# One PSUM bank and one copy for a chunk's value products, four score banks, spread-out maxima, and a new order for the attention stage

## The chip, the cores and the metric

The kernel runs on one core of one Trainium2 chip. The metric is the device time of one execution in microseconds (us). The kernel before took 383.84 us, the median of three runs (383.47, 383.84 and 385.26 us).

## The reference, cut to what matters

Three stages follow each other. Everything is float32, but `moe2_w_in` and `moe2_w_out`, which arrive as 8-byte floats and are converted on the chip.

```
q, k, v: (4 batches, 8 heads, 576 positions, 64)
scores = q k^T / 8                      # masked: heads 0-3 a window of the last 32 positions,
                                        # heads 4-7 every 4th of the last 128 positions
attn   = softmax(scores) ; a = attn v   # a, reordered: x of shape (2304, 512)
logits = x phi (512 x 32)               # softmax over all 2304 rows -> 32 slots of 512
slots  -> 8 experts: relu(slot w1) w2   # w1 8x512x1024, w2 8x1024x512
y      = softmax(logits, over slots) slot_out
out    = relu(y w_in)^2 w_out           # w_in 512x2048, w_out 2048x512
```

## The kernel before, in words

The changed part is the attention stage. It walks 24 **chunks**. A chunk is a pair of **units** (a unit is two heads of one batch) and a third of the positions: three blocks of 64 queries, each against 96 keys. Three chunks make a pair of units, six make a batch. A chunk has two **groups** (one for each head of the units), and these steps, each named by a letter:

- `q` (ch_qk, L342): the mask and the scores of both groups, one PSUM bank each. The pool `ps_s` has three banks, so the second of the next chunk's two score banks comes free only when the first group of the chunk has been exponentiated.
- `m` (ch_max, L366), once for each group: VectorE takes the row maxima, three numbers a row, negated.
- `c` (ch_sc, L372): VectorE multiplies the six maxima of a chunk by the scale 0.125, in place (L374).
- `x` (ch_exp, L376), once for each group: ScalarE's three exponentials (L381) with their sums.
- `r` (ch_rec, L386): VectorE adds 1e-9 to the six sums in place (L387) and takes the reciprocals (L388).
- `n` (ch_norm, L390), once for each group: the product with the reciprocals (L392), on GpSimd (`.g`) or VectorE (`.v`).
- `t` and `T`, once for each group: TensorE transposes (L400) into the one bank of `ps_t`, ScalarE or VectorE copies it out (L405).
- `p` (ch_pv, L408), once for each *unit*: the value products (L414) into a bank of `ps_v`, which has two banks.
- `P` (ch_pvev, L422), once for each unit: the copy into the ring `xring` of single-unit tiles, one copy (L432) for the window heads, two strided ones (L439) for the dilated heads.
- `d` (dup_v, L224), once for each unit of a chunk: 32 rows of v are copied to other partitions (L230), all by GpSimd.

When the six chunks of a batch are through, the router's work on the batch follows in the same queues: `X`/`Xe` transpose a unit's result (L452) and copy it out (L467), `L`, `Le`, `Lx`, `L2`, `D`, `De`, `Dx` make the logits and their exponentials, `S`/`Se` collect the slots, and `ce`, `cx`, `cn`, `cg` the second softmax.

The order of all this is written out by hand or by a planner in the string `ATT`: each engine executes its part of the tokens in exactly that order, and a token that waits holds up all that stand behind it on its engine. A token without a number takes the next of its kind, `t#27` is group 27. The last letter of a token chooses the engine or the PSUM pool. After the attention, `CL` closes the pools and issues the loads of the first chunks of `w_in` and `w_out` on the SP queue; the experts (`y`, L746, and `x`, L956) and the last stage (L1125, L1129, L1169, L1173) follow, by the string `SEQ`.

The loads are issued on the SP queue in a fixed order (P0, P1, P2, two w1 tiles, P3, two w1 tiles, ...; P is a pair's q, k and v), each as soon as a slot of the ring is free. `q` and `p` of a pair's last chunk free its slots for the weights of the experts.

Of the kernel before, what the change touches and what calls it, by code (L numbers as in the profile page):

```python
# [23 lines left out]
SCALE = 0.125  # L24
# [24 lines left out]
d Xe.a t r cx X.m m n.g T.a p m Xe.a c p n.g cn x t P.v S cg T.v x X.m d P.v q Se d Xe.v t r m X.m n.g T.a p m Xe.a
c p n.g P.v x t P.v S d x T.v q Se d t r X.m m n.g T.a p m Xe.a p c n.g P.v x t P.v p T.v x p d P.v q P.v d t r m S  # L50
n.g T.a m L c Se n.g x t#27 x Le q d T#27.v d Lx X.m r m t#26 n.g Xe.a p m T#26.a c X.m n.g L2.v x t P.v D Xe.v p x
De q d T.v P.a X.m r Dx m t n.g Xe.a m p T.a c n.g p ce x t P.v d S P.v x T.v q Se d cx t r p m n.g T.a m p P.a c
X.m n.g cn x t Xe.v X.m d p T.v x q P.v cg Xe.v P.a d t r p m n.g T.a m S P.a c n.g t x Se X.m d T.v X.m p Xe.v x q
# [39 lines left out]
def attn_softmoe_relu2_kernel(  # L93
# [84 lines left out]
    xring = [(ap1 if i < 4 else aq1).tile([128, S], F32, name=f"xr{i}") for i in range(6)]  # L178
# [45 lines left out]
    def dup_v(u, c):  # L224
# [5 lines left out]
        nc.gpsimd.tensor_tensor(  # L230
            v[:WIN, lo:3 * c + 3, :], v[QB:KB, lo - 1:3 * c + 2, :],
            zero[QB:KB, :n].unsqueeze(2).to_broadcast([WIN, n, 128]), op=ALU.subtract,
        )
# [132 lines left out]
    def ch_max(g):  # L366
        if g % 2 == 0:
            ng_t[g // 2] = ap3.tile([128, 12], F32, tag="ns", name="ns")
        ns = ng_t[g // 2]
        nc.vector.tensor_reduce(ns[:, 3 * (g % 2):3 * (g % 2) + 3], s_t[g], axis=AX.X, op=ALU.max, negate=True)  # L370

    def ch_sc(n):  # L372
        ng = ng_t[n][:, 0:6]
        nc.vector.tensor_scalar(ng, ng, SCALE, None, op0=ALU.mult)  # L374

    def ch_exp(g):  # L376
        p = p_t[g] = app.tile([128, 3, KB], F32, tag="p", name="p")
        ns, a = ng_t[g // 2], 3 * (g % 2)
        s, ng, sm = s_t.pop(g), ns[:, a:a + 3], ns[:, a + 6:a + 9]
        for i in range(3):  # L380
            nc.scalar.activation(  # L381
                p[:, i, :], s[:, i, :], AF.Exp, bias=ng[:, i:i + 1], scale=SCALE, accum_out=sm[:, i:i + 1]
            )
# [24 lines left out]
    def ch_pv(g):  # L408
        n, i = divmod(g, 2)
        u, c = units_of[n][i], units_of[n][2]  # L410
        o = ps_v.tile([128, 3, QB], F32, tag="v", name="o")
        for j in range(3):
            for h in range(2):
                nc.tensor.matmul(  # L414
                    o[64 * h:64 * h + 64, j, :],
                    lhsT=v_t[u][:, 3 * c + j, 64 * h:64 * h + 64],
                    rhs=pt_t[2 * n + h][:, j, QB * i:QB * i + QB],
                    start=True, stop=True,
                )
        pv_t[g] = o  # L420
        if c == 2:
            free(("load_kv", u))  # L422

    def ch_pvev(g, e):
        n, i = divmod(g, 2)
        u, c = units_of[n][i], units_of[n][2]
        b, kc = units[u]
        x = xT_t[b, kc] = xring[u % 6]
        o = pv_t.pop(g).rearrange("p i q -> p (i q)")
# [214 lines left out]
    def glob_w2():  # L644
# [712 lines left out]
```

## Time and profile before

| What | us |
|---|---|
| median of three runs | 383.84 |
| profiled execution | 382.7 |
| its span | 380.8 |
| busy TensorE / VectorE / ScalarE / GpSimd | 364.0 / 317.3 / 244.8 / 78.2 |
| first scores to the last attention exponential | 8.3 to 99.3 |
| first matmul of the experts | 114.9 |

The profiled execution took 382.7 us, of which 380.8 are the span from the first to the last instruction. The attention stage fills the first 105 us, the closing of the router some 9 more, the experts run to 143.6, and the rest is the last stage. TensorE's modelled busy time counts the pipeline's latency, so that 100% is not TensorE at its peak.

### The profile page before, as it was taken

How to read it: one execution, taken by the hardware profiler on the slowest of the kernel's cores; microseconds unless marked ns; L12 is line 12 of the kernel's file. 1: busy time of each engine (PE TensorE's matmuls, PEld its weight loads, DVE VectorE, ACT ScalarE, POOL GpSimd, SP SyncE). 2: the span in 40 equal slices, each digit the busy share in tenths (PEclk: the TensorE clock that was granted, in tenths of full speed). 3: DMA queues.
4: the chain of work that ended last, by engine and by line, in shares of the span. 5: the costliest groups of instructions: out<-in, count | busy, mean ns of one | idle time of the engine just before them, and what ended most of it. 6: DMA issues, size and time to landing. Idle time of an engine off the chain costs nothing.

```text
span 380.8 us, 9512 instructions
## 1 busy us (share of the span) xinstructions
PE 364.0 (96%) x3650; PEld 289.7 (76%) x3650; DVE 317.3 (83%) x681; ACT 244.8 (64%) x663; POOL 78.2 (21%) x161
## 2 busy tenths in 40 slices
PE   7878999999998998999999999999999999999995
PEld 3456777777763333777788788778999999999995
DVE  1768888988773237899999999999899999999984
ACT  3557787778644006899998686656966556465640
POOL 2788887674301020000000000120000000000000
PEclk9999999999999999999999999999999999999999
DMA  7999999998899999484753001300100101010101
GB/s 202 386 389 387 391 391 389 376 333 294 297 367 357 386 382 387 151 314 129 256 184 111 2 0 55 112 0 3 55 2 19 39 2 56 2 57 0 56 1 57
DMA packets 34460, 70.20 MB, mean 184 GB/s; under 512 B 2416, under 2 KB 6256, under 8 KB 34416
## 3 DMA queue, kind: packets, MB, share of 16 engines
q1 hardware_dynamic: 34272, 69.48, 50.9%
q8 instruction: 29, 0.48, 0.5%
q10 hardware_dynamic: 144, 0.13, 0.1%
q14 instruction: 15, 0.12, 0.1%
HBM read 64.88 MB, written 4.72 MB: 183 GB/s over the span
## 4 chain that ended last, share of the span: by engine, by line
PE 65%; DVE 16%; ACT 8%; DMA 4%; issue 4%; SPq 1%; POOL 1%; POOLq 0%; ACTq 0%; DVEq 0%
PE acc L1169 17%; PE acc L1173 8%; PE acc L1125 6%; PE o L414 4%; PE pt L400 4%; PE ph L1059 4%; ACT p L381 3%; DMA wi<-in_w_in_dram 3%; PE acc L1129 3%; PE pso L956 3%; PE xnp L452 2%; PE s L357 2%; DVE lo L1110 2%; PE psh L746 2%; PE ph L1008 2%
## 5 line engine op out<-in xcount | busy, mean ns | idle before, releaser
L1110 DVE TENSOR_TENSOR lo<-g,hi 128x896 fp32r<-128x896 f32 (+2 forms) x75 | 65.4, 873 | 3.3 <-ACT hi L1103 1.2
L1125 PE MATMUL acc<-hl,hi 128*128 128x512 f32 x256 | 67.8, 397 | 0.1
L1069 ACT ACTIVATE u<-ph 128x512 f32<-128x512 f32 (+1 forms) x75 | 42.3, 576 | 25.5 <-PE ph L1059 25.2
L381 ACT ACTIVATE p<-s,ns 128x96 f32<-128x96 f32 x144 | 46.8, 344 | 17.8 <-DVE ns L374 16.9
L1125 PEld LDWEIGHTS acc<-hl,hi 128*128 128x128 f32 x256 | 46.5, 188 | 10.1 <-ACT hi L1103 0.3
L1083 ACT ACTIVATE g<-u 128x512 f32<-128x512 f32 (+1 forms) x67 | 41.4, 620 | 13.9 <-DVE lo L1110 13.1
L1169 PE MATMUL acc<-hl,hi 128*128 128x256 f32 x296 | 48.7, 282 | 0.0
L1169 PEld LDWEIGHTS acc<-hl,hi 128*128 128x128 f32 x296 | 41.2, 188 | 0.0
L1169 PE MATMUL acc<-home,hi 128*128 128x256 f32 x219 | 40.2, 283 | 0.0
L1129 PE MATMUL acc<-hl,lo 128*128 128x512 f32 x128 | 38.0, 400 | 0.0
L700 POOL COPY c3n<-c_all 96x96 f32<-96x96 f32 x24 | 7.8, 359 | 131.6 <-PE ph L712 109.3
L1103 ACT CAST hi<-g 128x512 fp32r<-128x512 f32 (+2 forms) x40 | 29.9, 747 | 7.6 <-DVE g L1094 4.8
L392 POOL TENSOR_TENSOR p<-p,ns 128x288 f32<-128x288 f32 x43 | 27.9, 667 | 21.5 <-DVE ns L388 14.2
L1169 PEld LDWEIGHTS acc<-home,hi 128*128 128x128 f32 x219 | 32.3, 189 | 0.0
L1173 PE MATMUL acc<-hl,lo 128*128 128x256 f32 x148 | 30.2, 282 | 0.0
L381 ACT ACTIVATION_READ_ACCUMULATOR p<-s,ns 128x1 f32 x144 | 30.2, 210 | 0.0
L1129 PEld LDWEIGHTS acc<-hl,lo 128*128 128x128 f32 x128 | 23.4, 188 | 5.6 <-issue 0.4
L400 PE MATMUL pt<-ident,p 128*96 128x128 f32 x144 | 25.1, 283 | 0.9 <-POOL p L392 0.6
L1173 PE MATMUL acc<-home,lo 128*128 128x256 f32 x102 | 24.1, 282 | 0.0
L370 DVE TENSOR_REDUCE ns<-s 128x3 f32<-128x288 f32 x48 | 19.5, 442 | 5.4 <-PE s L357 5.4
L1093 DVE TENSOR_TENSOR g<-g 128x384 f32<-128x384 f32 x39 | 21.5, 552 | 2.7 <-ACT g L1083 2.5
L1173 PEld LDWEIGHTS acc<-hl,lo 128*128 128x128 f32 x148 | 23.6, 189 | 0.0
(217 smaller groups left out, 755.9 us busy)
## 6 DMA issues: line engine op xcount, KB each, us to landing
slotB<-in_w_dram SPq DMA_DIRECT2D x15, 1024.0 KB, 9.7
slotC<-in_w_dram SPq DMA_DIRECT2D x11, 1024.0 KB, 10.3
slotA<-in_w_in_dram SPq DMA_DIRECT2D x6, 1024.0 KB, 6.0
slotA<-in_w_out_dram SPq DMA_DIRECT2D x6, 1024.0 KB, 5.1
slotA<-in_w_dram SPq DMA_DIRECT2D x5, 1024.0 KB, 9.7
out_dram<-o SPq DMA_DIRECT2D x8, 512.0 KB, 2.8
slotC<-in_kq_dram SPq DMA_DIRECT2D x14, 288.0 KB, 8.2
slotB<-in_kq_dram SPq DMA_DIRECT2D x10, 288.0 KB, 9.8
```

The source lines that it names most:

```text
L381: nc.scalar.activation(p[:, i, :], s[:, i, :], AF.Exp, bias=ng[:, i:i + 1], scale=SCALE, accum_out=sm[:, i:i + 1])
L392: {"v": nc.vector, "g": nc.gpsimd}[e].tensor_tensor(p, p, rs.unsqueeze(2).to_broadcast([128, 3, KB]), op=ALU.mult)
L400: nc.tensor.transpose(pt[:, i, :], p[:, i, :], ident)
L1069: nc.scalar.activation(r, u_t[k][:, :n], AF.Relu)
L1083: nc.scalar.activation(out, r, AF.Square)
L1093: E.tensor_tensor(runs(g, 128, 384, 3, 128), runs(g, 0, 384, 3, 128), runs(g, 384, 384, 3, 128), op=ALU.add)
L1103: on(e.lower())(hi[:, :c.stop - c.start], g_t[k][:, c])
L1110: nc.vector.tensor_tensor(lo[:, :n], g_t.pop(k)[:, c], hi_t[k][:, :n], op=ALU.subtract)
L1125: nc.tensor.matmul(a, lhsT=hi_t[k][:, sl], rhs=hl_t[q][:, x, j], start=(fs[0] == 0 and i == 0 and x == 0), stop=False)
L1129: nc.tensor.matmul(a, lhsT=lo_t[k][:, sl], rhs=hl_t[q][:, 0, j], start=False, stop=(fs[-1] == 15 and i == len(fs) - 1))
L1169: nc.tensor.matmul(a, lhsT=hi_t[k][:, sl], rhs=right(q, w, x), start=(q == 0 and x == 0 and i == 0), stop=False)
L1173: nc.tensor.matmul(a, lhsT=lo_t[k][:, sl], rhs=right(q, w, 0), start=False, stop=(q == (6 if p == LP and nm != "Z" else 7) and i == len(PR ...
```

## The change

`ps_s` gets four banks and `ps_v` one. `p` now runs both units' products into one bank (24 matmuls in one run), `P` copies both with one copy (or two strided ones), into ring tiles that hold two units. `c` writes the six scaled maxima to another place of the same tile, as three pairs four columns apart, and the exponentials take their biases from there; `r` writes its sums through that place too, and the reciprocals go back. `d` can be done by ScalarE (`.a`), and 23 of 48 are. `q` chooses its pool by token. The order is written anew, with every token numbered.

```
+q#0.s m#0 m#1 c#0 x#0 q#1.s x#1 q#2.m m#2 d#4.g d#2.a r#0 W d#0.a m#3 d#5.g n#0.v d#1.a d#3.a n#1.g t#1 c#1 m#4 x#3
+m#5 T#1.v x#2 c#2 t#0 x#5 T#0.v d#6.g r#1 p#0 x#4 n#2.g P#0.v q#3.s d#8.g d#7.a r#2 t#2 d#10.a n#3.g m#6 T#2.a m#7
+q#4.s n#4.g d#9.a c#3 t#3 x#7 m#8 n#5.g T#3.v q#5.m x#6 d#11.g m#9 t#4 m#10 m#11 p#1 c#4 T#4.a r#3 d#12.g x#9 t#5
...
...
-    ps_s = att.enter_context(tc.tile_pool(name="ps_s", bufs=3, space=PSUM))
+    ps_s = att.enter_context(tc.tile_pool(name="ps_s", bufs=4, space=PSUM))
-    ps_v = att.enter_context(tc.tile_pool(name="ps_v", bufs=2, space=PSUM))
+    ps_v = att.enter_context(tc.tile_pool(name="ps_v", bufs=1, space=PSUM))
-    xring = [(ap1 if i < 4 else aq1).tile([128, S], F32, name=f"xr{i}") for i in range(6)]
+    xring = [(ap1 if i < 2 else aq1).tile([128, 2, S], F32, name=f"xr{i}") for i in range(3)]
...
+        if e == "a":
+            nc.scalar.copy(dst, src)
+        else:
+            nc.gpsimd.tensor_tensor(
+                dst, src, zero[QB:KB, :n].unsqueeze(2).to_broadcast([WIN, n, 128]), op=ALU.subtract,
+            )
...
+    def pairs_of(n):
+        return ng_t[n][:, 12:24].rearrange("p (a b) -> p a b", b=4)[:, :, 0:2]
     def ch_sc(n):
-        ng = ng_t[n][:, 0:6]
-        nc.vector.tensor_scalar(ng, ng, SCALE, None, op0=ALU.mult)
+        nc.vector.tensor_scalar(pairs_of(n), ng_t[n][:, 0:6], SCALE, None, op0=ALU.mult)
...
-        rs = ng_t[n][:, 6:12]
-        nc.vector.tensor_scalar(rs, rs, 1e-9, None, op0=ALU.add)
-        nc.vector.reciprocal(rs, rs)
+        rs, r2 = ng_t[n][:, 6:12], pairs_of(n)
+        nc.vector.tensor_scalar(r2, rs, 1e-9, None, op0=ALU.add)
+        nc.vector.reciprocal(rs.rearrange("p (a b) -> p a b", b=2), r2)
...
+    def ch_pv(n):
+        u0, u1, c = units_of[n]
+        o = pv_t[n] = ps_v.tile([128, 2, 3 * QB], F32, tag="v", name="o")
+        for i, u in enumerate((u0, u1)):
+            for j in range(3):
+                for h in range(2):
+                    nc.tensor.matmul(
+                        o[64 * h:64 * h + 64, i, QB * j:QB * j + QB],
+                        lhsT=v_t[u][:, 3 * c + j, 64 * h:64 * h + 64],
+                        rhs=pt_t[2 * n + h][:, j, QB * i:QB * i + QB],
+                        start=True, stop=True,
+                    )
+            if c == 2:
+                free(("load_kv", u))
+    def ch_pvev(n, e):
+        u0, u1, c = units_of[n]
+        x = xring[u0 // 2 % 3]
...
+        if units[u0][1] < 2:
+            on(e)(x[:, :, lo:hi], o)
             return
...
+            dst = x.rearrange("p i (t r) -> p i t r", r=DIL)[:, :, t0:t0 + z - a, r]
+            on(e)(dst, o[:, :, a - lo:z - lo])
```

Of the tokens that choose an engine, the new order has these numbers (before in brackets): `n` on VectorE 1 (5), `T` on ScalarE 25 of 48 (24), `Xe` on ScalarE 14 of 32 (16), `L2` on ScalarE 4 of 4 (1), `P` on ScalarE 5 of 24 (12 of 48, each half as large), `d` on ScalarE 23 of 48 (0). In VectorE's order before, `c` of every chunk stood behind `r` of the chunk before it. In the new order it stands ahead of that `r` for 12 of 23 chunks (2, 4, 5, 6, 7, 9, 11, 12, 15, 17, 20, 23) and behind it for the others.

## Rows read from the trace of the kernel before

**Rows 1.** The page: modelled TensorE busy tenths and HBM traffic, 40 slices of 9.52 us.

```profile
PE  7878999999998998999999999999999999999995
GB/s 202 386 389 387 391 391 389 376 333 294 297 367 357 386 382 387 151 314 129 256 184 111 2 0 55 112 0 3 55 2 19 39 2 56 2 57 0 56 1 57
```

**Rows 2.** Windows: stretch, its length, then busy us (instructions) of each engine.

```profile
8.30:47.75 39.45, 33.89 (x568) 23.61 (x568) 29.73 (x89) 26.04 (x135) 31.75 (x56) 1.00 1.04 387
47.75:99.30 51.55, 50.67 (x999) 39.59 (x999) 45.70 (x151) 42.43 (x213) 34.15 (x57) 1.00 0.96 344
99.30:105.50 6.20, 6.20 (x105) 4.58 (x104) 4.11 (x14) 3.31 (x10) 1.61 (x3) 1.00 1.04 370
```

**Rows 3.** ScalarE's waits from 8 to 48 us: total us, times, longest.

```profile
ACT p L381 <- DVE ns L374: 14.9, 10, 5.8
ACT pts L405 <- PE pt L400: 4.3, 9, 0.7
```

**Rows 4.** ScalarE's waits from 48 to 100 us.

```profile
ACT pts L405 <- PE pt L400: 5.2, 8, 1.0
ACT p L381 <- DVE ns L374: 2.4, 7, 0.4
ACT xn L467 <- PE xnp L452: 0.9, 2, 0.5
```

**Rows 5.** Timeline around chunk 2: start us, us, instruction, [idle before it].

```profile
13.85 0.17 DVE L387 TENSOR_SCALAR ns<-ns 128x6 f32<-128x6 f32 x1 [0.76 <-ACT p L381]
14.49 0.90 DVE L392 TENSOR_TENSOR p<-p,ns 128x288 f32<-128x288 f32 x1
15.79 0.31 DVE L374 TENSOR_SCALAR ns<-ns 128x6 f32<-128x6 f32 x1
16.20 0.34 ACT L381 ACTIVATE p<-s,ns 128x96 f32<-128x96 f32 x1 [1.51 <-DVE ns L374]
```

**Rows 6.** The line L374: ns minimum/median/maximum of one instruction.

```profile
L374 DVE TENSOR_SCALAR ns<-ns x24: 170/190/841, 8.0 to 97.0; 128x6 f32<-128x6 f32 x24
```

**Rows 7.** The group of L374 by line: busy us, mean ns of one, idle before.

```profile
L374 DVE TENSOR_SCALAR ns<-ns 128x6 f32<-128x6 f32 x24 | 8.3, 346 | 0.8
```

**Rows 8.** Timelines of GpSimd and VectorE around one slow L374, and GpSimd's first copy.

```profile
73.11 1.29 POOL L392 TENSOR_TENSOR p<-p,ns 128x288 f32<-128x288 f32 x2 [1.05 <-DVE ns L388]
73.78 0.65 DVE L374 TENSOR_SCALAR ns<-ns 128x6 f32<-128x6 f32 x1
...
10.06 1.39 POOL L230 TENSOR_TENSOR slotC<-slotC,zero 32x256 f32<-32x256 f32 x2 [5.54 <-DMA slotC<-in_vw_dram]
```

**Rows 9.** ScalarE's groups from 8.3 to 99.3 us: busy us, mean ns of one.

```profile
L405 ACT COPY pts<-pt 96x384 f32<-96x384 f32 x22 | 10.4, 474 | 9.5 <-PE pt L400 9.4
L439 ACT COPY xr<-o 128x144 f32<-128x144 f32 (+2 forms) x9 | 2.5, 372 | 0.0
L432 ACT COPY xr<-o 128x192 f32<-128x192 f32 x5 | 1.6, 327 | 0.1
L546 ACT ACTIVATE lc<-lc 96x192 f32<-96x192 f32 x3 | 1.1, 375 | 0.0
```

**Rows 10.** Timeline of VectorE: one copy of a window chunk's two, a dilated chunk's four.

```profile
51.91 0.31 DVE L432 COPY xr<-o 128x192 f32<-128x192 f32 x1
55.11 0.85 DVE L439 COPY xr<-o 128x144 f32<-128x144 f32 x4 [0.17 <-PE o L414]
```

**Rows 11.** The line L405: ns minimum/median/maximum of one copy.

```profile
L405 DVE COPY pts<-pt x24: 537/550/555, 12.5 to 102.7; 96x384 f32<-96x384 f32 x24
```

**Rows 12.** The chain that ended last, behind the attention: start us, us, what.

```profile
105.75 12.17 DMA wi<-in_w_in_dram
122.16 0.49 ACT hs L761
```

**Rows 13.** The SP queue's own waits: total us, times, longest.

```profile
SPq L247 <- PE s L357: 10.4, 1, 10.4
SPq L247 <- PE o L414: 7.9, 3, 6.5
```

More of the change, by code (lines that the diff above doesn't have):

```diff
@@ L49 @@
[L49 to L53, printed above, removed]
@@ L59 @@
-fsp cx S Se w1 S w2 Se st Se S cn ste.a st st Se cg ste.a st ste.a ste.a
+q#0.s m#0 m#1 c#0 x#0 q#1.s x#1 q#2.m m#2 d#4.g d#2.a r#0 W d#0.a m#3 d#5.g n#0.v d#1.a d#3.a n#1.g t#1 c#1 m#4 x#3
+m#5 T#1.v x#2 c#2 t#0 x#5 T#0.v d#6.g r#1 p#0 x#4 n#2.g P#0.v q#3.s d#8.g d#7.a r#2 t#2 d#10.a n#3.g m#6 T#2.a m#7
+q#4.s n#4.g d#9.a c#3 t#3 x#7 m#8 n#5.g T#3.v q#5.m x#6 d#11.g m#9 t#4 m#10 m#11 p#1 c#4 T#4.a r#3 d#12.g x#9 t#5
+P#1.v q#6.s n#6.g T#5.v x#8 d#16.g c#5 t#6 m#12 T#6.a p#2 m#13 n#7.g x#10 c#6 d#13.g r#4 P#2.v t#7 T#7.a n#8.g q#7.s
@@ new lines @@
+d#17.a p#3 m#14 n#9.g x#11 m#15 d#15.g c#7 t#9 X#1.m d#14.a P#3.v T#9.a X#2.m r#5 x#13 t#8 Xe#1.v n#11.g T#8.v X#0.m
+x#12 n#10.g Xe#2.v t#11 Xe#0.v T#11.a p#4 r#6 x#14 P#4.v t#10 n#12.g q#8.s T#10.a n#13.g d#18.a t#12 m#16 x#15 d#22.g
+p#5 T#12.v m#17 d#20.a t#13 r#7 d#23.g d#19.a c#8 X#3.m T#13.v P#5.a n#14.g q#9.s n#15.g t#14 x#16 m#18 p#6 T#14.v
+m#19 d#21.a t#15 P#6.v x#17 L#0 T#15.v c#9 r#8 x#18 n#17.g Le#0 p#7 x#19 n#16.g t#17 P#7.v T#17.a q#10.s r#9 Lx#0 t#16
+n#18.g m#20 L2#0.a T#16.a D#0 m#21 n#19.g c#10 Dx#0 De#0 q#11.s d#24.g x#21 ce#0 p#8 m#22 x#20 d#26.g t#18 m#23 c#11
@@ new lines @@
+S#0 d#27.g P#8.v d#25.a q#12.s T#18.a r#10 Xe#3.a Se#0 n#21.g x#23 m#24 t#19 S#1 n#20.g T#19.v x#22 X#4.m Se#1 d#28.g
+t#20 m#25 Xe#4.v p#9 T#20.a c#12 cx#0 r#11 t#21 x#25 d#29.g n#22.g cn#0 X#5.m X#11.m T#21.v x#24 n#23.g q#13.s Xe#5.v
+cg#0 t#22 P#9.v Xe#11.a S#2 T#22.a r#12 p#10 Se#2 n#24.g m#26 t#23 m#27 n#25.g P#10.a X#6.m c#13 T#23.v X#7.m d#30.g
+x#26 q#14.s Xe#6.v Xe#7.v d#34.g t#25 x#27 m#28 S#3 T#25.v d#32.g Se#3 p#11 d#31.a r#13 d#33.g d#35.a q#15.s m#29
+n#26.g P#11.v t#24 n#27.g X#8.m c#14 T#24.v x#28 L#1 m#30 Xe#8.a m#31 x#29 c#15 t#26 Le#1 p#12 x#30 T#26.v r#14 t#27
@@ new lines @@
+P#12.v X#9.m n#28.g Lx#1 T#27.v x#31 q#16.s Xe#9.v n#29.g t#28 m#32 L2#1.a q#17.s m#33 T#28.a r#15 t#29 c#16 n#31.g
+d#36.a m#34 D#1 T#29.v d#38.a X#12.m n#30.g De#1 Dx#1 p#13 x#32 m#35 c#17 t#30 d#39.g P#13.v d#37.a S#4 x#33 T#30.v
+d#40.g Se#4 p#14 ce#1 Xe#12.a d#41.g P#14.a t#31 r#16 X#10.m T#31.a X#18.m n#33.g cx#1 Xe#10.v p#15 x#35 n#32.g cn#1
+t#32 P#15.v x#34 cg#1 S#5 T#32.a Se#5 q#18.s r#17 Xe#18.a t#33 n#35.g m#36 X#13.m T#33.a m#37 X#14.m Xe#13.v n#34.g
+t#35 c#18 x#37 S#6 T#35.v p#16 Se#6 d#44.a d#46.g d#42.a Xe#14.v P#16.v t#34 x#36 X#15.m X#19.m Xe#15.v q#19.s d#43.a
@@ new lines @@
+d#47.g T#34.a r#18 S#7 n#37.g d#45.a m#38 m#39 p#17 Se#7 n#36.g c#19 Xe#19.a x#38 t#37 P#17.v q#20.s T#37.a L#2 m#40
+x#39 m#41 c#20 x#41 r#19 t#36 Le#2 n#38.g X#17.m T#36.a Xe#17.v q#21.s x#40 n#39.g t#38 m#42 p#18 T#38.a m#43 r#20
+Lx#2 c#21 t#39 n#40.g x#42 P#18.v X#16.m T#39.v n#41.g q#22.s L2#2.a t#41 x#43 m#44 p#19 T#41.v r#21 D#2 m#45 t#40
+P#19.a n#42.g De#2 Dx#2 T#40.a q#23.s n#43.g c#22 ce#2 x#45 S#9 m#46 t#43 m#47 Xe#16.a Se#9 x#44 c#23 p#20 T#43.v S#8
+P#20.a r#22 x#46 t#42 Se#8 n#45.g X#20.m T#42.v X#22.m n#44.g X#25.s x#47 Xe#20.v t#45 Xe#22.v p#21 T#45.a r#23 cx#2
@@ L60 @@
+n#46.g P#21.v t#44 X#23.m n#47.g T#44.a X#21.m Xe#23.a cn#2 X#24.s t#46 p#22 T#46.a cg#2 t#47 P#22.v S#11 T#47.a Se#11
+Xe#24.a X#26.s p#23 Xe#21.v P#23.v La CL S#10 Xe#25.v Lb Se#10 Xe#26.a X#28.m Le#3 X#29.s Xe#28.v Lx#3 X#27.s g X#30.s
+L2#3.a D3 Xe#27.a X#31.s ff De3 Dl S#12 Xe#31.a Dle fs ce#3 Xe#29.a fsp Se#12 S#13 cx#3 w1 w2 S#14 Xe#30.a Se#13 Se#14
+st#0 S#15 cn#3 ste#0.a st#2 st#1 Se#15 ste#1.a cg#3 ste#2.v st#3 ste#3.v
 """
@@ L222, in attn_softmoe_relu2_kernel, with dup_v @@
     v0 = []
-    def dup_v(u, c):
+    def dup_v(u, c, e):
         v = v_t[u]
@@ L229, in dup_v @@
         n = 3 * c + 3 - lo
[L230 to L233, printed above, removed]
+        dst, src = v[:WIN, lo:3 * c + 3, :], v[QB:KB, lo - 1:3 * c + 2, :]
+        if e == "a":
[4 more added lines that the diff above has]
+            )
     w1_t, w2_t, wi_raw, wo_raw, wo_hl = {}, {}, {}, {}, {}
@@ L378, in ch_exp @@
         ns, a = ng_t[g // 2], 3 * (g % 2)
[L379 removed]
+        s, ng, sm = s_t.pop(g), pairs_of(g // 2), ns[:, a + 6:a + 9]
         for i in range(3):
             nc.scalar.activation(
[L382 removed]
+                p[:, i, :], s[:, i, :], AF.Exp, bias=ng[:, (a + i) // 2, (a + i) % 2:(a + i) % 2 + 1], scale=SCALE,
+                accum_out=sm[:, i:i + 1],
             )
     def ch_rec(n):
[L386 to L388 removed]
+        rs, r2 = ng_t[n][:, 6:12], pairs_of(n)
+        nc.vector.tensor_scalar(r2, rs, 1e-9, None, op0=ALU.add)
+        nc.vector.reciprocal(rs.rearrange("p (a b) -> p a b", b=2), r2)
     def ch_norm(g, e):
@@ L406, in ch_tev @@
         pt_t[g] = t
[L408 to L429, printed above, removed]
+    def ch_pv(n):
[15 more added lines that the diff above has]
+        x = xring[u0 // 2 % 3]
+        for i, u in enumerate((u0, u1)):
+            xT_t[units[u]] = x[:, i, :]
+        o = pv_t.pop(n)
         lo, hi = 192 * c, 192 * c + 192
-        if kc < 2:
-            on(e)(x[:, lo:hi], o)
+        if units[u0][1] < 2:
+            on(e)(x[:, :, lo:hi], o)
             return
```

21 lines of the change are left out of this document (4 added, 17 removed).

## Prediction

> **What bounds the kernel now.** I read the page's slices first: TensorE is below nine tenths in the first four slices, and HBM traffic, at 390 GB/s from the second slice on, drops to 333, 294 and 297 GB/s in slices 9 to 11, the second half of the attention [rows 1]. The last stage behind it is full and untouched by the change. So the question is when the attention ends, and what hangs on that. The windows then split the attention at 47.75 us, where the exponentials of chunk 10 begin, and at 99.3 us, where the last ones end [rows 2]. In the first part TensorE works 33.9 of 39.5 us and ScalarE 26.0; in the second TensorE 50.7 of 51.6, ScalarE 42.4, VectorE 45.7. No engine is full in the first part: it is bound by latency. ScalarE's waits say by which. Up to 48 us it waits 14.9 us for the scaled maxima of L374 (5.8 of them before the very first exponential at 8.3 us, so 9.1 count) and 4.3 us for transposes to copy out [rows 3]; after 48 us only 2.4 us for L374, and 5.2 + 0.9 us for TensorE [rows 4].
>
> The timeline shows the loop behind the 9.1 us. The exponentials of chunk 1 end at 13.8, then VectorE does r (13.85), one row maximum, a normalisation of 0.90 us (14.49), the other row maximum, and only then c (15.79), which lets chunk 2's exponentials start at 16.20, after 1.51 us of idling [rows 5]. Two things force it: c stands behind the r of the chunk before it, which needs that chunk's last exponential, and with three score banks the second group's scores can't be written earlier.
>
> ScalarE is therefore the ledger in which I add up: from 8.3 to 99.3 us are 91.0 us, 26.0 + 42.4 = 68.5 of work [rows 2], 22.5 of idling. The named waits nearly fill it: 9.1 + 2.4 = 11.5 for VectorE's L374, 4.3 + 5.2 + 0.9 = 10.4 for TensorE, 0.6 for others.
>
> **The change, part by part.**
>
> *Copies of v on ScalarE (d).* 23 are added to its queue: 12 of 384 columns, 11 of 256. The trace has none there. A PSUM copy of 384 columns takes 0.474 us, of 192 columns 0.327, and an instruction that reads 192 columns from SBUF 0.375 [rows 9], so I add 0.05 for SBUF: 0.52 and, between, 0.42 us. Neighbours overlap: nine strided copies of 0.372 us, 3.35 in all, fill only 2.5, so 0.09 each [rows 9]. That gives 12 x 0.43 + 11 x 0.33 = 8.8 us. The bounds are 0, if every one falls into idle time, and 12 x 0.52 + 11 x 0.42 = 10.9. I take 8.8 as work and count idle time apart. GpSimd, busy 31.8 + 34.2 of 91.0 [rows 2], gives up these 23 and gets four more normalisations; it is no bound before or after. The first ScalarE copies stand ahead of chunk 1's exponentials and can wait for v to land. GpSimd's first two started at 10.06 when a load released them [rows 8], about when ScalarE is through with chunk 0's exponentials (8.3 + 2); I take 0.5 us for it, between 0 and 2.
>
> *One product bank, one copy (p, P).* The 24 matmuls stay. A window chunk's two VectorE copies take 0.31 us each, a dilated chunk's four 0.85 [rows 10]; one copy of 384 columns takes 0.55 [rows 11]. The strided merged pair lies between 0.55 and 0.85; I take 0.85, the nearest row with that stride, so a window chunk saves 0.07 and a dilated one nothing: 12 x 0.07 = 0.8 us of VectorE as I take it, at most 12 x 0.3 more, at least nothing. On VectorE, which works 29.7 + 45.7 of 91.0 us [rows 2], this is beside the path. ScalarE had 2.5 + 1.6 = 4.1 us of these copies [rows 9] and gets three of 0.39 and two of about 0.95 (VectorE's 0.85 and a tenth, an estimate): -1.0. [...] With one bank, a chunk's products wait for the copy of the chunk before. A chunk takes 51.55 / 14 = 3.7 us in the second part [rows 2] and the copy follows its products at once, well ahead of the next run, which hides it; without that cover it costs 0.55 to 0.95 us a chunk.
>
> *Other moves on ScalarE* up to its last exponential: T 22 to 21 (-0.4), Xe 9 to 7 (-0.8), L2 0 to 3 (3 x 0.25 = +0.8). ScalarE's work thus rises by 8.8 - 1.0 - 0.4 - 0.8 + 0.8 = 7.4, to 75.9 us.
>
> *Four score banks and the new order.* c stands ahead of the older r for 12 of 23 chunks, five of chunks 1 to 7. So the scores, maxima and c of such a chunk are done while the exponentials before it run, and the loop of 1.5 us is gone there. In the other cases ScalarE has v copies, T or P to do meanwhile. Of the 11.5 us I leave 2.0 (bounds 0 and 11.5; most of the loss lies early, where the look-ahead is fullest). Of the 10.4 us for TensorE I leave 8.3: all of the late ones, where TensorE is full, and half of the early 4.3. What comes late next is TensorE: with the same work and no idling it needs 33.9 + 50.7 = 84.6 of these 91.0 us, so this stage can give at most 6.4 us by the page's busy time.
>
> *Scaled maxima in another place (c, r).* L374 takes 170 ns at best, 190 in the median and up to 841 [rows 6]. A slow one, 0.65 us from 73.78, ends at 74.43, as the normalisation that GpSimd began before it ends (73.11 + 1.29 = 74.40) [rows 8]: VectorE waits for GpSimd's instruction. The excess over the best, 24 x (346 - 170) ns, is 4.2 us [rows 7]. [...] What they bring ScalarE is inside the 11.5 us above; where c is early they bring nothing. The new shape itself, still six columns, I cost at nothing, with 24 x (190 - 170) ns = 0.5 us as the bound above, beside the path where c is early.
>
> *Normalisations on VectorE* fall from five to one: 4 x 0.9 us, early, of the loop above [rows 5], also inside the 11.5.
>
> *Sum.* Idle time 2.0 + 8.3 + 0.6 + 0.5 = 11.4 in place of 22.5, work +7.4: 22.5 - 11.4 - 7.4 = 3.7 us earlier at the last exponential. From there to the router's logits are 6.2 us in which TensorE is full [rows 2]; the new order leaves about as many transposes and products behind the last exponential, so I add nothing. The profiled execution (382.7, span 380.8) would take 379.0; the median of the runs shown is 1.1 above it, so 383.84 - 3.7 = 380.1.
>
> *Does the rest follow?* Behind the attention the chain goes through a load: wi, issued at 105.75, lands 12.17 us later, and ScalarE, whose queue has that chunk's conversion ahead of the experts' relu, reaches the relu at 122.16 [rows 12]. The slices give 36.5 MB up to 104.7 us (their first eleven, 3835 x 9.52 us) and at 367 GB/s 4.9 MB more up to 117.9. With the slow first slice (1.9 MB) and no gap at 390 GB/s behind it these 41.4 MB are there at 9.5 + 39.5 / 0.39 = 110.7: wi can come at most 7.2 us earlier. That is enough for 3.7.
>
> **The rivals.**
>
> *ScalarE becomes the bound (slower).* All 23 v copies stand in its queue ahead of exponentials, with T and P copies that wait for TensorE. In the ledger the new order loses as soon as more than 91.0 - 75.9 = 15.1 us of idling are left, and by over 0.5% from 17.0 on. For it: 22.5 are there now, and TensorE's share of 10.4 need not fall where TensorE is full. Against it: the early 9.1 us have a plain cause that the order removes. With 18.5 us left the time is 383.84 + 3.4 = 387.2.
>
> *The gain is hidden by the load.* The weights wait for slots: SP waits 10.4 us for scores and 7.9 us for products [rows 13], and the new order runs products two to three chunks behind scores, so v's slots come free later against the rest. If wi lands no earlier, the relu stays at 122.16 and the time at 383 to 384. Against it: the last products must still end earlier with the stage.
>
> *The spread-out write changes nothing.* If L374 still loses 4.2 us to GpSimd, the 11 of 23 chunks with c behind r keep 2.0 of it on ScalarE's path, and the time is 380.1 + 2.0 = 382.1.
>
> *A larger gain.* With TensorE's waits gone as well, TensorE's 6.4 us and the load's 7.2 are the limits: 376.5 to 377.5, below that only if TensorE's pitch falls too.
>
> **How the numbers follow.** Something over 0.5% (1.9 us) is what a measurement tells from no change. The forecast (377.5 to 381.9, by waits left between 8.9 and 13.2) 0.54, larger gain 0.13: faster 0.67. Hidden load 0.12 and unchanged lock 0.06: same 0.18. ScalarE as the bound 0.15: slower 0.15. The likeliest's own range is 377.5 to 381.9; the range reaches down to 375.8 for the larger gain and up to 385.5, short of the slower rival.
>
> **What would show it.** ScalarE's waits for L374 up to 48 us fall to 2 us besides the first; chunk 10's exponentials start near 43; the last exponential ends near 95.5; wi lands near 114; L374's maximum is below 300 ns; v copies on ScalarE take 0.42 and 0.52 us. It would be wrong if ScalarE idles over 15 us between its first and last exponential, if a product run waits for P's copy in most chunks, or if the experts don't start earlier by what the exponentials gained.

## Result, and the profile after

The changed kernel takes 377.96 us, the median of four runs (376.91 to 378.77), beside 383.65 us for the kernel before on the same chip (383.01 to 385.26). The ratio is 0.9844, with a 95% interval from 0.9805 to 0.9883: faster, by 5.7 us where 3.7 were forecast, and inside the likeliest range. The profiled execution of the changed kernel took 378.77 us, the slowest of its four, with a span of 376.8 us; against the profiled execution of before (382.7, 380.8) it gained 3.9 us, of the span 4.0. Where the two traces are set side by side, it is these 4.0 us that are explained. Medians here and below are of all executions, while ratios and intervals leave out executions that were over 1.5% slower than the fastest of their kernel, so that a ratio need not be the quotient of two medians.

The page's slices answer to [rows 1]: busy tenths of TensorE, the granted clock, and HBM traffic, in 40 slices of 9.42 us.

```profile
PE   6799999999997998999999999999999999999995
PEclk9999999999998999999999999999999999999999
GB/s 204 384 386 390 390 393 388 391 384 374 356 383 387 386 377 350 108 230 197 247 183 43 2 0 105 64 0 2 57 3 56 2 2 56 3 57 0 57 0 58
```

TensorE is at nine tenths from the third slice on instead of the fifth, and the dip of the traffic in slices 9 to 11 (333, 294 and 297 GB/s before) is shallow now (384, 374 and 356). In slice 13, from 113 us on, TensorE and its granted clock have a dent; it is taken up below.

The windows, cut where they were cut before [rows 2], at the first exponential, at the first of chunk 10, and at the end of the last:

```profile
7.28:41.31 34.03, 29.46 (x592) 21.56 (x596) 23.51 (x73) 31.27 (x149) 22.01 (x42) 1.00 1.04 383
41.31:93.25 51.94, 50.16 (x994) 38.68 (x988) 43.12 (x136) 44.49 (x215) 29.75 (x51) 1.00 1.05 386
```

The columns after the length are TensorE, its weight loads, VectorE, ScalarE and GpSimd. The stage is 86.0 us long instead of 91.0. All of that is in the first part, 34.0 instead of 39.5 us; the second part has 51.9 instead of 51.6. ScalarE works 31.27 + 44.49 = 75.8 us, so it idles 10.2.

ScalarE's waits in the first part answer to [rows 3] (total us, times, longest):

```profile
ACT p L397 <- DVE ns L390: 5.6, 2, 4.8
ACT slotC L244 <- DMA slotC<-in_vw_dram: 1.1, 1, 1.1
ACT pts L422 <- PE pt L417: 0.3, 1, 0.3
```

Of the 5.6 us for the scaled maxima (L390, L374 before), 4.8 lie ahead of the first exponential, so 0.8 is left of 9.1. The waits for transposes fall from 4.3 to 0.3. In the second part, by the view that answers to [rows 4], L390 costs 1.5 us. TensorE costs 1.4 us for transposes and 1.9 us for products (`xr <- o`), which ScalarE did not wait for before:

```profile
ACT pts L422 <- PE pt L417: 1.4, 2, 0.9
ACT p L397 <- POOL p L409: 1.2, 1, 1.2
ACT p L397 <- DVE ns L390: 1.1, 2, 0.6
ACT xr L455 <- PE o L431: 1.0, 1, 1.0
ACT xr L448 <- PE o L431: 0.9, 2, 0.8
ACT lc L550 <- DVE dn L544: 0.8, 1, 0.8
ACT lc L550 <- DVE ns L390: 0.4, 1, 0.4
```

The lines of the changed operations answer to [rows 6, 10] (ns minimum/median/maximum of one instruction): the scaled maxima, the v copies on ScalarE, and the merged product copies on VectorE.

```profile
L390 DVE TENSOR_SCALAR ns<-ns x24: 116/150/168, 7.0 to 89.9; 128x6 f32<-128x6 f32 x24
L244 ACT COPY slotC<-slotC x13: 397/503/513, 9.4 to 65.6; 32x384 f32<-32x384 f32 x7, 32x256 f32<-32x256 f32 x6
L455 DVE COPY xr<-o x20: 310/516/715, 26.3 to 99.0; 128x288 f32<-128x288 f32 x7, 128x96 f32<-128x96 f32 x7, 128x192 f32<-128x192 f32 x6
L448 DVE COPY xr<-o x9: 546/558/558, 15.6 to 83.9; 128x384 f32<-128x384 f32 x9
```

No scaling takes longer than 168 ns any more. By the timelines of VectorE and GpSimd, some of them end while an instruction of GpSimd beside them runs on: the scaling at 26.22 us ends at 26.38 and GpSimd's copy, begun at 26.17, at 26.99; the scaling at 23.52 us ends at 23.68 and GpSimd's normalisation, begun at 23.24, at 23.91. A v copy takes 0.50 us for 384 columns and 0.40 for 256.

Behind the attention the chain answers to [rows 12] (start us, us, what):

```profile
101.36 10.58 DMA wi<-in_w_in_dram
...
112.05 0.69 ACT cv L854
...
116.09 0.49 ACT hs L777
116.58 0.04 issue
116.62 3.62 PE psh L762 x16
```

and TensorE's timeline of the experts' start shows what hangs on it, before (first two lines) and after:

```profile
114.88 3.64 PE L746 MATMUL psh<-slotB,slotT 128*32 128x512 f32 x32 [0.32 <-issue]
122.70 1.07 PE L746 MATMUL psh<-slotC,slotT 128*32 128x512 f32 x8 [0.75 <-ACT hs L761]
...
107.51 3.64 PE L762 MATMUL psh<-slotB,slotT 128*32 128x512 f32 x32 [0.49 <-DVE slotT L611]
110.94 1.93 PE L762 MATMUL psh<-slotA,slotT 128*32 128x512 f32 x16
112.66 1.93 PE L762 MATMUL psh<-slotC,slotT 128*32 128x512 f32 x16
116.62 1.92 PE L762 MATMUL psh<-slotC,slotT 128*32 128x512 f32 x8 [2.04 <-ACT hs L777]
118.31 1.94 PE L762 MATMUL psh<-slotB,slotT 128*32 128x512 f32 x8
```

The experts begin 7.4 us earlier (107.51 for 114.88). But wi lands only 6.0 us earlier (111.94), and ScalarE reaches the relu (L777) 6.1 us earlier, so TensorE waits 2.04 us for it where it waited 0.75. After this wait eight matmuls take 1.92 us, as long as sixteen took just before, and the windows show the clock:

```profile
112.00:116.00 4.00, 2.59 (x26) 0.63 (x16) 2.24 (x4) 2.42 (x5) 0.00 (x0) 1.00 1.05 386
116.00:118.00 2.00, 1.38 (x8) 0.40 (x12) 0.69 (x1) 1.06 (x3) 0.00 (x0) 0.67 1.06 389
118.00:120.00 2.00, 2.00 (x12) 0.21 (x4) 0.00 (x0) 0.00 (x0) 0.00 (x0) 0.50 1.04 384
```

From 118 to 120 us the granted share (the third column from the end) is 0.50. The sixteen matmuls on the chain took 3.62 us, where the sixteen at 112.66 took 1.93: 1.7 us more. So of the 7.4 us, 1.3 are lost to the longer wait and 1.7 to the clock. That leaves 4.4; 4.0 reach the end, and where the last 0.4 go I did not trace. The loss to the clock belongs to this execution: in the profiled execution of the control below TensorE waits 1.47 us at this place, and the eight matmuls behind take 1.07 us.

### The profile page after: what moved, and what is told of

Its sections match the earlier page's. It is cut to its first block, busy times and chain, and to the rows that moved or that the text cites. A ratio compares the mean times of both kernels' runs of the same rounds, so it can differ in the third digit from the quotient of the medians.

```text
span 376.8 us, 9464 instructions
## 1 busy us (share of the span) xinstructions
PE 359.0 (95%) x3650; PEld 286.4 (76%) x3650; DVE 309.1 (82%) x653; ACT 251.5 (67%) x674; POOL 64.5 (17%) x142
## 4 chain that ended last, share of the span: by engine, by line
PE 66%; DVE 14%; DMA 6%; issue 5%; ACT 4%; SPq 2%; POOL 2%; POOLq 0%; DVEq 0%; ACTq 0%
PE acc L1185 17%; PE acc L1189 9%; PE acc L1141 6%; PE pt L417 5%; PE o L431 4%; PE ph L1075 4%; PE acc L1145 3%; DMA wi<-in_w_in_dram 3%; PE pso L972 3%; PE psh L762 3%; PE s L371 2%; PE xnp L468 2%; DMA slotC<-in_vw_dram 2%; DVE lo L1126 2%; PE pacc L580 2%
## 5 line engine op out<-in xcount | busy, mean ns | idle before, releaser
L409 POOL TENSOR_TENSOR p<-p,ns 128x288 f32<-128x288 f32 x47 | 30.6, 669 | 28.1 <-DVE ns L405 9.7
L1109 DVE TENSOR_TENSOR g<-g 128x384 f32<-128x384 f32 x39 | 21.6, 554 | 2.7 <-ACT g L1099 2.5
```

The costliest lines, as they stand in the source:

```text
L409: {"v": nc.vector, "g": nc.gpsimd}[e].tensor_tensor(p, p, rs.unsqueeze(2).to_broadcast([128, 3, KB]), op=ALU.mult)
L1109: E.tensor_tensor(runs(g, 128, 384, 3, 128), runs(g, 0, 384, 3, 128), runs(g, 384, 384, 3, 128), op=ALU.add)
```

## The experiments

Three accounts of the gain stood against each other; the expectations say what would follow. By the first, it comes from the new order of the early chunks, and what holds back the rest is the load wi, the relu behind it and the clock. By the second, it comes from one of the parts: the v copies, the spread-out maxima or the banks. By the third, the prediction's own, it comes within the order from c standing ahead of the older r. All ratios are to the kernel before, run beside the experiment.

**The control**, the changed kernel again.

> The changed kernel again, as the control of the three beside it. Every theory: 377 to 379 us, ratio to before 0.981 to 0.988. The first exponential began 1.0 us earlier in its first profile, behind the same commands; if that was chance, this profile has it anywhere between 7.2 and 8.4 us.

Measured: 378.11 us, ratio 0.9859 (0.9814 to 0.9904). It agrees with the first measurement.

**The maxima in place again**, in the new order.

```
-        nc.vector.tensor_scalar(pairs_of(n), ng_t[n][:, 0:6], SCALE, None, op0=ALU.mult)
+        nc.vector.tensor_scalar(ng_t[n][:, 0:6], ng_t[n][:, 0:6], SCALE, None, op0=ALU.mult)
```

> The changed kernel with c and r writing in place again (six adjacent columns). Theory A (the gain comes from the order and the fourth score bank, which let c run ahead): L374's counterpart costs about 4 us of VectorE again, but where c is early this is hidden; 0 to 2 us slower than the control, 378 to 380. [...]

Measured: 378.18 us, 0.9849 (0.98 to 0.9898). Slow scalings are back, up to 872 ns:

```profile
L390 DVE TENSOR_SCALAR ns<-ns x24: 130/172/872, 7.7 to 93.4; 128x6 f32<-128x6 f32 x24
```

In the new order they cost nothing that can be measured; the intervals are wide enough to hide up to some 2 us.

**The spread-out maxima alone**, in the kernel before.

```
-        ng = ng_t[n][:, 0:6]
-        nc.vector.tensor_scalar(ng, ng, SCALE, None, op0=ALU.mult)
+        nc.vector.tensor_scalar(pairs_of(n), ng_t[n][:, 0:6], SCALE, None, op0=ALU.mult)
```

> The kernel before with one part of the change: c and r write the spread-out place. Theory A: L374's excess of 4 us goes, but only its part on ScalarE's path counts: the early chunks lose 0.1 to 0.7 us each; 0.5 to 2.5 us faster than before (381 to 383). [...] If the new place does not keep VectorE out of GpSimd's way, L374's maximum stays at 0.6 us or more and the time at before's.

Measured: 382.71 us, 0.9948 (0.9909 to 0.9987), some 2.0 us. The scalings take 160 ns at most:

```profile
L376 DVE TENSOR_SCALAR ns<-ns x24: 118/159/160, 7.9 to 95.2; 128x6 f32<-128x6 f32 x24
```

In the old order, where c stands in ScalarE's loop, the slow scalings were worth about 0.5%.

**All 48 v copies on GpSimd**, in the places planned for ScalarE (`d#0.a` to `d#0.g` and so on, 23 times).

> The changed kernel with all 48 copies of v on GpSimd again, in the places where the new order has them. Theory A, by ScalarE's ledger: 23 copies, about 9 us of ScalarE's work, go, and if GpSimd keeps up the last exponential ends 1 to 4 us earlier (374 to 378). Theory C (the copies had to leave GpSimd, since normalisations queue behind them): GpSimd's busy time rises from 22 to some 30 of the first 34 us, ScalarE waits for transposes again, 1 to 4 us slower than the control (379 to 382).

Measured: 385.32 us, 1.0036 (1.0012 to 1.0061): the whole gain is gone. ScalarE's waits up to 48 us are long again:

```profile
ACT p L397 <- DVE ns L390: 9.7, 3, 5.8
ACT pts L422 <- PE pt L417: 4.8, 3, 2.7
ACT p L397 <- DVE ns L404: 3.1, 1, 3.1
```

The first part (the granted clock in it, 0.91, is the third column from the end):

```profile
8.23:47.50 39.27, 31.57 (x584) 23.16 (x588) 23.03 (x73) 25.80 (x136) 31.40 (x54) 0.91 1.04 385
```

By itself this would speak for the v copies on ScalarE. But a copy in GpSimd's queue in a place that was chosen for another engine also holds up the normalisations behind it: in this part TensorE waits 5.8 us for GpSimd's normalisations, where it waited 0.5 us in the changed kernel. The maxima and c stand where they stand in the changed kernel, so their place alone does not make the gain.

**All 48 on GpSimd, in places of their own**: d#0 to d#3 behind m#1, and the two copies of each later chunk behind the second normalisation of the chunk two before it; everything else in the changed kernel's order.

```
-q#0.s m#0 m#1 c#0 x#0 q#1.s x#1 q#2.m m#2 d#4.g d#2.a r#0 W d#0.a m#3 d#5.g n#0.v d#1.a d#3.a n#1.g
+q#0.s m#0 m#1 d#0.g d#2.g d#1.g d#3.g c#0 x#0 q#1.s x#1 q#2.m m#2 r#0 W m#3 n#0.v n#1.g d#4.g d#5.g
```

> The changed kernel with all 48 copies of v on GpSimd, placed anew: each chunk's two behind the normalisations of the chunk two before it, so that they need not stand ahead of an urgent normalisation. Theory F (they cost that much on GpSimd only because they stood where ScalarE's had been planned): at most 1 us slower than the changed kernel, or faster by ScalarE's 9 us of work (375 to 379). Theory D (GpSimd has no room for them in the early chunks): 3 to 7 us slower than the changed kernel, 381 to 385, with GpSimd over 30 us busy from 8 to 48 us.

Measured: 378.1 us, 0.9866 (0.9833 to 0.9899), as fast as the changed kernel. The places make the difference of 7 us to the run before, not the engine. Its windows:

```profile
8.04:42.85 34.81, 30.54 (x584) 22.34 (x588) 23.10 (x73) 25.50 (x136) 28.72 (x50) 0.95 1.04 382
42.85:93.67 50.82, 49.63 (x994) 38.52 (x984) 43.45 (x136) 40.33 (x206) 39.16 (x66) 1.00 1.05 387
```

ScalarE works 10 us less (65.8), idles 10 us more (19.8), and the stage has the same length, 85.6 us. So ScalarE does not set it. In the second part TensorE is busy for 49.6 of 50.8 us.

**The v copies alone**, the same 23 on ScalarE, in the kernel before.

> The kernel before with one part of the change: the same 23 copies of v on ScalarE, in the old order, nothing else. Theory D (that GpSimd gave up these copies is the main cause, since all the gain went without it): normalisations come earlier, 2 to 5 us faster than before (379 to 382). Theory E (the copies are room that only the new order can use): ScalarE gets 9 us more work ahead of exponentials that wait for c as before, -1 to +4 us (383 to 388).

Measured: 386.13 us, 1.0068 (1.0042 to 1.0094): alone they cost.

**The banks and the merged products alone**, in the old order (the second `p` and `P` of each chunk left out of the string).

```
-    ps_s = att.enter_context(tc.tile_pool(name="ps_s", bufs=3, space=PSUM))
+    ps_s = att.enter_context(tc.tile_pool(name="ps_s", bufs=4, space=PSUM))
-    ps_v = att.enter_context(tc.tile_pool(name="ps_v", bufs=2, space=PSUM))
+    ps_v = att.enter_context(tc.tile_pool(name="ps_v", bufs=1, space=PSUM))
```

> The kernel before, in its old order, with four score banks, one product bank, and one run and one copy for both units' products (at the place of the second unit's). Theory A (banks without the order that uses them give nothing, since c still stands behind r): within 2 us of before, 382 to 386, with ScalarE's early waits for L374 still over 6 us. Rival (the third bank was the limit): ScalarE's early waits halve and the time is 379 to 381.

Measured: 388.87 us, 1.0055 (1.0008 to 1.0102), a little slower than before, and the early waits for the maxima are 7.1 us besides the first. The fourth bank is no gain while nothing uses it to look ahead.

**c behind r**, in the changed kernel, for all the 12 chunks in which the new order has it ahead; nothing else is moved.

```
-q#0.s ... m#5 T#1.v x#2 c#2 t#0 x#5 T#0.v d#6.g r#1 p#0 ...
+q#0.s ... m#5 T#1.v x#2 t#0 T#0.v d#6.g r#1 c#2 x#5 p#0 ...
```

> The changed kernel with c put right behind the r of the chunk before it, in the 12 chunks where the new order has it ahead; nothing else is moved on any engine. Theory A (c ahead of r is what ended the early waits): ScalarE's waits for c return, about 1 us in each of the 5 early chunks and up to 0.5 in the others, 3 to 7 us slower than the control (381 to 385). Rival (four banks, or the v copies that fill ScalarE's queue, did it, and the place of c is without weight): within 1 us of the control.

Measured: 378.47 us, 0.9862 (0.9827 to 0.9898): the step has no weight, and the prediction's own account falls. VectorE's timeline, at chunk 4, shows why:

```profile
19.59 1.18 DVE L382 TENSOR_REDUCE ns<-s 128x3 f32<-128x288 f32 x3
20.95 0.16 DVE L402 TENSOR_SCALAR ns<-ns 128x6 f32<-128x6 f32 x1 [0.17 <-ACT p L395]
21.14 0.19 DVE L403 RECIPROCAL ns<-ns 128x6 f32<-128x6 f32 x1
21.25 0.12 DVE L388 TENSOR_SCALAR ns<-ns 128x6 f32<-128x6 f32 x1
```

The row maxima (L382) were done before r (L402, L403), so c (L388) starts 0.3 us after r does. It is so in all 15 of 23 chunks whose two maxima stand ahead of the older r in the new order: 0.28 to 0.32 us from the start of r to that of c. In the other eight it is 1.1 to 1.8 us, and in the kernel before 1.1 to 1.95 us in all but chunk 1. ScalarE's waits for c do come back in part (2.3 + 4.2 us in the two parts besides the first wait, where the changed kernel has 0.8 + 1.5), yet the time stays.

**All parts in the old order**: spread-out maxima, four banks, merged products and the 23 v copies on ScalarE. Only the new order is missing.

> All parts of the change in the old order: spread-out c and r, four score banks and one product bank, one run and one copy for both units' products, the 23 copies of v on ScalarE. Only the new order is missing. If the order is the cause: 382 to 388, most of the changed kernel's gain is gone. If the parts make the gain and the order only arranges them: 378 to 380.

Measured: 387.07 us, 1.0076 (1.0033 to 1.0118). Without the order the parts together cost 3 us. VectorE's timeline, at chunk 3, is that of [rows 5] again:

```profile
18.04 0.16 DVE L401 TENSOR_SCALAR ns<-ns 128x6 f32<-128x6 f32 x1 [0.69 <-ACT p L394]
18.24 0.19 DVE L402 RECIPROCAL ns<-ns 128x6 f32<-128x6 f32 x1
18.35 0.42 DVE L381 TENSOR_REDUCE ns<-s 128x3 f32<-128x288 f32 x1
18.68 0.90 DVE L406 TENSOR_TENSOR p<-p,ns 128x288 f32<-128x288 f32 x1
19.50 0.44 DVE L381 TENSOR_REDUCE ns<-s 128x3 f32<-128x288 f32 x1
19.98 0.16 DVE L387 TENSOR_SCALAR ns<-ns 128x6 f32<-128x6 f32 x1
```

Between r and c stand both maxima and a normalisation: 1.9 us from the start of r to the start of c. ScalarE's waits for c here are 3.5 us in the first part besides the first (9.1 before) and those for transposes 6.7 (4.3 before), so the loop, though it is back, is not the largest part of the loss. The windows:

```profile
8.15:51.47 43.32, 36.99 (x566) 26.93 (x567) 26.09 (x78) 32.52 (x149) 20.99 (x39) 0.72 1.04 387
51.47:103.51 52.04, 49.31 (x990) 38.10 (x990) 42.05 (x136) 46.83 (x217) 28.45 (x49) 1.00 0.87 308
```

The first part is 43.3 us, 9.3 more than in the new order, and ScalarE idles 10.8 of it. The granted clock there is 0.72, so some of this is the clock and not the order's own: the same part of the kernel before, 39.5 us at 1.00, took 41.7 us at 0.92 in the run below that only moves its relus, and that of the changed kernel, 34.0 us at 1.00, took 36.9 us at 0.91 in the control. But its fastest run, at a mean clock of 0.991, took 383.52 us, where the kernel before beside it had a median of 383.77: in this one run at a good clock, too, the parts give nothing.

**The relus first**, in the changed kernel: the first expert's two relus (`r.A`) and its transposes go ahead of the conversions of the first chunks of w_in and w_out.

```
-y i0.0A i0.1A y y i0.2V y i0.3V y i0.4V y o0.0A o0.1A y o0.2V y o0.3V r.A y y t.V y r.A o0.4V cp
+y y y y r.A y y y y t.V r.A i0.0A i0.1A y y y i0.2V i0.3V i0.4V o0.0A o0.1A o0.2V o0.3V o0.4V cp
```

> The changed kernel with the experts' first two relus ahead of the conversion of the first w_in and w_out chunks in every queue; nothing in the attention is touched. [...] Rival (the later weights are the bound: HBM is full until about 145 us): the matmuls only wait for w2 later, within 1 us of the changed kernel.

Measured: 377.03 us, 0.9794 (0.9736 to 0.9852). The experts' first 64 matmuls now run without a gap; the chain has them as one piece:

```profile
106.82 7.07 PE psh L762 x64
```

But the experts' gain is partly given back. From 140 to 150 us, where the last matmuls of the experts stand (in the kernel before they end at 149, not at 143.6), TensorE is less busy than in the changed kernel (8.78 us there, at 1.00), and its clock falls:

```profile
140.00:150.00 10.00, 7.02 (x28) 6.14 (x28) 5.98 (x13) 5.49 (x13) 0.00 (x0) 0.66 0.97 368
```

The gain on the changed kernel is about 1 us, where I had expected 2 to 4, an estimate from the wait of 2.04 us and the 1.7 us of slow matmuls, and the intervals overlap, so it is not shown to be faster than that. In this trace TensorE waits 2.25 us (to 142.23) for the copy-out of the experts' second output; by the chain, a load of a chunk of w_out that lands at 140.70 stands ahead of it.

**The same move in the kernel before.**

> The kernel before with the same move of the first two relus. [...] Theory A: 0.5 to 1 us faster than before (382.5 to 383.2), so that most of what the move gives the changed kernel is a price that the earlier end of the attention has brought. Rival: it gives the kernel before as much as the changed one.

Measured: 382.16 us, 0.9952 (0.9919 to 0.9985). It gains at least as much there (1.8 us by the ratio), so the wait for the relu is not only a price of the change: before, too, a conversion that waits for wi stood ahead of it. The 0.75 us of that wait do not account for all of the 1.8; the rest I did not trace.

**A version to beat both**: the relus first, and the copy-out of the experts' second output and its selection (`so.AV`, `sel.A`) ahead of a conversion of w_out.

```
-x i2.2V o2.1A x P1 s0.0V s1.0A o2.0V so.AV i3.1A s0.1V s1.1V sel.A P2
+x i2.2V x P1 so.AV sel.A o2.1A s0.0V s1.0A o2.0V i3.1A s0.1V s1.1V P2
```

> The changed kernel with the first two relus ahead of the first conversions, and with the experts' last copy-out and selection ahead of the third w_out chunk's conversion in ScalarE's queue. With the relus alone TensorE still waited 2.3 us there and its clock fell to 0.66 of full speed in the stretch from 140 to 150 us. If that wait was only a place in the queue, 2 to 4 us faster than the relus alone, 373 to 375.5; if the weights' landing bounds the experts and the last stage anyway, within 1 us of them, 376 to 378.

Measured: 376.39 us, 0.9818 (0.9785 to 0.9851). TensorE's wait for the copy-out falls from 2.25 to 0.49 us and the granted clock from 140 to 150 us is 1.00 again, so this wait was a place in the queue. But the time is within 1 us of the relus alone, as was expected if the landing of the weights is the bound. It has the lowest median of all, though not the lowest ratio (0.9794, the relus alone), and is faster than the kernel before. Its interval overlaps those of the changed kernel (0.9844 and 0.9859), so that it beats this one too is not shown.

## Why the prediction was right, and which step failed

*The ledger came out right in its totals, and not in all its terms.* ScalarE's work was forecast at 75.9 us and is 75.8; its idling at 11.4, and it is 10.2. But of the idling TensorE's share is 3.6 us where 8.3 were left: 1.7 for transposes, and 1.9 for products, which I had at nothing. The waits for c are 2.3 us for 2.0, the wait for v 1.1 for 0.5, and 3.2 us go to others (GpSimd's normalisations, the router, short gaps) where I had 0.6. That the sum fits is in part these errors offsetting each other. Chunk 10 was to start near 43 and starts at 41.3; the last exponential was to end near 95.5 and ends at 93.25. Of this, 1.0 us is the first exponential's earlier start (7.28 instead of 8.31): in the profiles of the runs with the new order it starts between 7.17 and 8.23, so I don't count it as the change's. wi was to land near 114 and landed at 111.94, since the stage gained more than forecast and the load had room for 7.2.

*The step that failed* is the one on four score banks and the new order: that the loop of 1.5 us goes because "c stands ahead of the older r for 12 of 23 chunks". With c behind r for all of them the time stays (378.47). What the runs show in its place: the gain is in the new order as a whole, since all the parts in the old order give nothing (387.07), and in it the two maxima of 15 of 23 chunks stand ahead of the r of the chunk before (of one chunk in the old order), so that from the start of r to that of c are 0.3 us in place of 1.1 to 1.95. I had the loop right in [rows 5] and then picked one instruction of it, the last, instead of the two maxima and the normalisation that stood between r and c. That the forecast time was met although this step was wrong is luck: the loop went, for another reason than mine.

That the maxima are this reason is read from the traces and not shown by a run that moves only them back. The chain that ended last, followed back through the trace, gives the loop in the kernel before: of the 39.5 us of the first part it has 14.7 of VectorE and 12.4 of ScalarE's exponentials, one after the other, and of the 14.7 the maxima are 5.4, r 3.3, c 2.8 and normalisations 2.5. VectorE has 2.8 us of it in the changed kernel and 4.0 with c behind r, but only 5.5 with all parts in the old order too, where TensorE at the lower clock takes 21.6; so the chain does not settle it. Nor does a run show that the fourth bank is needed. It alone gives nothing (388.87), but none has the new order with three, and the scores of chunks 2 and 5 take the two banks of `ps_m` (`q#2.m`, `q#5.m`). None has the new order without the merged products either. How the gain divides among the moves of the order, the scores ahead, fewer normalisations on VectorE, the router's work earlier, stays open.

*The slow scalings* (the "unchanged lock" of the chances). That the 4.2 us would go with the spread-out write was my estimate, and no run shows by what it comes about. The runs show the times: at most 168 ns in the changed kernel and 160 with the spread-out write in the kernel before, up to 872 with the maxima in place again. "Where c is early they bring nothing" is not contradicted in the new order (in place again: 378.18), for all chunks and not only the 12, as far as intervals of half a per cent tell. In the old order the spread-out write brings 2.0 us of the 4.2 by which I measured the excess. The rival that it changes nothing falls as to the scalings: 841 ns became 168.

*The v copies* are priced right (0.50 and 0.40 us for 0.52 and 0.42), and the wait for v to land was 1.1 us for 0.5. But the ledger had me count them as a loss of 8.8 us, and taken away they give nothing (378.1). ScalarE's first part shows it, work + idle = length, in us:

| kernel | work | idle | length | granted clock |
|---|---|---|---|---|
| before | 26.0 | 13.4 | 39.5 | 1.00 |
| changed | 31.3 | 2.8 | 34.0 | 1.00 |
| changed, the control | 31.6 | 5.3 | 36.9 | 0.91 |
| v copies on GpSimd, in ScalarE's places | 25.8 | 13.5 | 39.3 | 0.91 |
| v copies on GpSimd, placed | 25.5 | 9.3 | 34.8 | 0.95 |
| all parts, old order | 32.5 | 10.8 | 43.3 | 0.72 |

With the new order, the copies in places of their own and a granted clock of 0.95 or more, the length is 34 to 35 us with much or little work on ScalarE. A sum of work and waits along one engine comes out right for any execution, and does not say that this engine is the bound. What bounds these 34 us no run settles. By the chain that ended last they are 6.6 us of a load of v that lands at 15.38, 15.9 us of TensorE and 4.8 us of GpSimd, and little else. The second part is 50.8 to 53.0 us in all six, with TensorE at 49.3 to 50.7, as the prediction had it. Its floor of 84.6 us for TensorE's busy time was none, though: after the change it is 79.6 us. Of the 5.0 us between, 4.6 are the value products' (24.4 us before, 19.8 after). In the second part, at a granted clock of 1.00, TensorE's modelled busy time for one of these matmuls is 42 to 43 ns where 12 stand in a run (before, and with the v copies alone) and 38 ns where 24 do (changed, and with all parts in the old order), so this goes with the merged runs and not with the order.

*One product bank, one copy.* On VectorE the merged copy of a window chunk takes 0.56 us (forecast 0.55), and that of a dilated one 8.6 us for ten chunks, 0.86 (0.85). Two strided copies in place of four that stood next to each other save nothing here.

*Does the rest follow?* By less than forecast, and this was hidden in the profiled sum: the experts start 7.4 us earlier, the span ends 4.0 earlier. The 7.4 are 1.0 of the earlier start, 5.0 of the stage, and 1.3 between the last exponential and the experts' first matmul (14.3 us for 15.6), where I had added nothing. The load's room of at most 7.2 us was held against 3.7. At 7.4 it is not enough: wi comes 6.0 us earlier, TensorE's longer wait for the relu costs 1.3 us, and in this execution 1.7 us of clock. So the 3.9 us of the profiled pair came close to 3.7 by two errors that offset each other, a stage that gained more and an end that followed less. The medians, 5.7 us apart, have the typical runs: the changed kernel's profiled one was its slowest, and the profiled one of before was faster than each of the three runs shown with it.

*The rivals.* ScalarE did not become the bound: it idles 10.2 us, below the 15.1 from which it would have lost. The gain was not hidden by the load, but clipped by it. The larger gain, 376.5 to 377.5 us, lies next to the result, and by its own reason, TensorE's waits gone as well: those on ScalarE's side for transposes fell from 9.5 to 1.7 us. The two ranges meet at 377.5, so the time does not tell this rival from the forecast.

## What to carry to other kernels

In a loop over in-order queues, list everything that stands between the instruction that waits and the one that releases the next round. Here the place of the last one was worth nothing once the others stood ahead. A buffer more, and work moved to another engine, were worth nothing until the order used them, and an instruction moved to another queue needs a place chosen for that queue (7 us here). A ledger of one engine's work and waits sized this stage well in its total, with errors in its terms that offset each other; that the engine is the bound has to be shown by taking work off it.

## What the runs showed of the hardware that I had not expected

After a wait of 2.04 us behind a stretch at a granted clock of 1.00, TensorE's granted clock fell to 0.50, and matmuls that had taken 1.93 us for sixteen took 3.62 on the chain. The 0.75 us that it waited there in the kernel before had no such price, nor had waits of 1.38, 1.47, 1.69 and 1.96 us in four other profiles (c behind r, the control, and the v copies on GpSimd, placed and not): eight matmuls took 1.07 us there. In the old order with all parts, the first 43 us had a mean grant of 0.72, against 1.00 for the kernel before in nearly the same order: which part of that is cause and which is effect I did not test. Strided copies from PSUM were dearer here than plain ones: 288 columns into places four apart took 0.684 us in the mean on VectorE and up to 0.715, where 384 contiguous columns took 0.558 in the median.
